# New opening and closing order lists for a fused Linformer attention and feed-forward kernel

## The chip, the core and the metric

The kernel runs on one core of one Trainium2 chip. The metric is device time in microseconds (us) of one execution; lower is better. A profile records one execution: its span runs from the first to the last instruction. The engines are PE (TensorE matmuls), PEld (TensorE weight loads), DVE (VectorE), ACT (ScalarE), POOL (GpSimd, which here mostly issues the input transfers) and SP (which here issues the output and the small internal transfers).

## What is computed

Attention whose keys and values are projected from 1024 positions to 64, and then a feed-forward block on the concatenated heads:

```python
k_proj = einsum('ks,bhsd->bhkd', E, k);  v_proj = einsum('ks,bhsd->bhkd', F, v)
scores = matmul(q, k_proj^T) / sqrt(64)
attn   = softmax(scores, axis=-1)
x      = matmul(attn, v_proj)            # (8, 8, 1024, 64) -> 8192 tokens x 512
h      = x @ w_in                        # 8192 x 2048
out    = (h * sigmoid(1.702 * h)) @ w_out    # 8192 x 512
```

There are 8 batches, 8 heads, 1024 positions and a head size of 64. Inputs and output are float32; the matmuls run in bfloat16.

## The kernel before

**Blocks.** The 8192 tokens are cut into 16 blocks of 512 tokens, numbered 0 to 15. Block j belongs to batch j // 2, so a new batch starts at every even j. Each block goes through attention and then through the two feed-forward products. From block 2 on the first product, and from block 1 on the second, use the Strassen-Winograd scheme: seven half-size products in place of eight, and sums and copies on DVE and ACT between them. Blocks 0 and 1 use plain products where the summed weights are not ready yet.

**Steps.** All work is cut into small named steps. `step(name, j, banks, eng)` emits the instructions of one step for block j. A word such as `xt.0@2:4` means step `xt.0` of block 2 with its result in PSUM bank 4; `/A` or `/D` puts a copy on ACT or on DVE. The steps are:

| step | engine | what it does |
|---|---|---|
| `pj`, `kb`, `kt`, `kc`, `vq`, `vx` | PE, then copies | project keys and values of a new batch, transpose the keys, copy them out |
| `qt`, `qc` | PE, copy | transpose the queries of a block, copy them out |
| `sc`, `ex` | PE, ACT | scores; exponential |
| `tk`, `tr`, `tm`, `xt`, `xc` | PE, DVE, DVE, PE, copy | attention output of blocks 1 and 2, token-major: product, reciprocal, scaling, transpose, copy |
| `su`, `den`, `ga`, `rc`, `sr`, `sb` | PE, copy, SP, DVE, SP, SP | softmax sums of blocks 3 to 15: sum, copy, regroup by DMA (`rc<-den`), reciprocal, write (`rdr<-rc`), broadcast by DMA (`rbc<-rdr`) |
| `va`, `mv` | PE, DVE | attention output of these blocks; scaling by `rbc` |
| `xs` | DVE | sums of the attention output for the first product |
| `L`, `Lg` | PE, ACT | plain first product of block 1; its activation |
| `uN.P1` to `uN.P7`, `uN.c1` to `c3`, `uN.d1`, `d2`, `uN.g11` to `g22` | PE, copies, DVE, ACT | the seven products of quarter N (0 to 3), copies and sums between them, activations |
| `gs` | DVE | sums of the activations for the second product |
| `O`, `oc` | PE, copy | plain second product of block 0; copy to the output tile |
| `F1` to `F7`, `f3`, `f5`, `Fc1` to `Fc3`, `Fo`, `Fd`, `fd2`, `fc3` | PE, copies, DVE | Strassen-Winograd second product; copies and sums |
| `ws`, `wi` | DVE or ACT | sums of the weights `w_out` and `w_in` |
| `gt` | ACT | load the activation table of the feed-forward activation |
| `st*`, `s0` | SP | store output |
| `ld`, `lq` | POOL | load keys and values, or queries, of the next batch |

**Order.** The order is written out in lists. A preamble in code does block 0's attention and first product. After that `listed(OPEN)` emits the 547 words of the list `OPEN`; a loop over j = 4 to 12 emits the list `STEPS`, in which `+n` shifts a step to block j + n; and `listed(TAIL)` emits the 248 words of the list `TAIL`. Each engine executes its own instructions strictly in the order of emission. Across engines an instruction waits only for what it needs: data, or the last reader of a buffer or PSUM bank that it overwrites. So a word's place matters only against other words of the same engine; for the waits, the number of words of other engines ahead of it does.

**The Strassen-Winograd copies.** Within a quarter `uN`, `c1` copies the result of P1 to a second bank before P2 adds onto the first and P6, P7 and P4 add onto the second; `c2` must read that bank between P6 and P7; `c3` must read the third bank between P5 and P3; `d1` must come between P7 and P4. In the second product `Fc1` must copy the first bank after both halves of F1 and before F2 adds onto it. Each of these is a place where PE waits for ACT or DVE.

**Fixed order outside the lists.** POOL's queue holds, after the preamble, `ld@2`, `lq@2`, `ld@4`, `lq@4` and so on: `ld` waits until `pj` of the batch has read the old keys and values, and `lq` until the last `qt` of the batch has read the old queries.

Of the kernel before, what the change touches and what calls it, by code (L numbers as in the profile page):

```python
# [17 lines left out]
def kernel(ctx, tc, q, k, v, E, F,  # L18
# [251 lines left out]
    xs = {}  # L270
# [107 lines left out]
    def ffn2_ops(j):  # L378
# [8 lines left out]
        O.3.0@0:7 wi.4@1 sc.1@1:2,6 sc.0@1:1,0 ex.0.1@1 ex.0.0@1 O.2.0@0:3 O.2.1@0 O.3.1@0 tk.1.0@1:5 ex.1.0@1  # L387
        tk.0.0@1:4 tk.0.1@1:0 O.0.0@0:1 O.1.0@0:2 tr.0.1@1 ex.1.1@1 gt@3 tm.0.1@1 tr.0.0@1 tk.1.1@1:6 O.3.2@0
        tr.1.1@1 O.3.3@0 tm.0.0@1 tk.2.1@1:0 tm.1.1@1 xt.0@1:6 O.0.1@0 tr.2.1@1 tr.1.0@1 tm.1.0@1 tm.2.1@1
        oc.3@0/A xt.1@1:7 tk.2.0@1:5 tk.3.0@1:0 O.0.2@0 xc.0@1/A tr.2.0@1 tm.2.0@1 tk.3.1@1:5 O.2.2@0 O.1.1@0  # L390
        O.2.3@0 tr.3.0@1 ws.0@1 tr.3.1@1 tm.3.0@1 xc.1@1/A tm.3.1@1 ws.2@1 oc.2@0/D xt.3@1:7 xt.2@1:4 O.1.2@0
        ws.1@1 O.1.3@0 xc.2@1/A xc.3@1/A O.0.3@0 L.6@1:5 L.7@1:7 L.8@1:3 oc.1@0/D L.2@1:4 Lg.7@1 Lg.8@1 Lg.6@1
        qt.0@2:6 pj@2:2 oc.0@0/A qc.0@2/A vq.0@2/D L.5@1:5 L.1@1:0 L.11@1:7 L.0@1:3 vq.1@2/A gt@4 Lg.2@1 Lg.5@1
        kb@2/D L.3@1:1 Lg.3@1 L.10@1:6 L.12@1:4 Lg.1@1 Lg.11@1 Lg.0@1 Lg.12@1 L.4@1:0 wi.5@1/D Lg.10@1 vx.0@2
        vx.1@2 Lg.4@1 L.13@1:2 ws.3@1 L.9@1:4 kt@2:7 Lg.13@1 L.15@1:1 ws.4@1 gs3.1@1 kc@2 sc.0@2:3,7 Lg.9@1
        Lg.15@1 qt.1@2:5 ex.0.0@2 s0.0@0 qc.1@2/D ld@2 qt.0@3:2 qt.1@3:4 qc.1@3/D sc.1@2:1,6 ex.1.1@2 tk.0.1@2:4
        ex.0.1@2 ex.1.0@2 gt@1 tk.0.0@2:5 qc.0@3/D tr.0.0@2 L.14@1:6 tk.1.1@2:2 tk.1.0@2:0 tm.0.0@2 tr.0.1@2
        tm.0.1@2 tr.1.0@2 tk.2.0@2:7 Lg.14@1 lq@2 xt.0@2:5 tm.1.0@2 tr.1.1@2 tm.1.1@2 sc.0@3:4,3 tk.3.0@2:0
# [414 lines left out]
```

## Time and profile before

| what | value |
|---|---|
| time, median of 3 runs | 480.43 us (480.08 to 480.87) |
| the profiled execution: time, and its span | 481.29 us, 479.5 us |
| mean granted TensorE clock | 0.999 |
| DVE busy | 347.9 us (73%), 633 instructions |
| ACT busy | 325.1 us (68%), 561 instructions |
| POOL busy | 81.2 us (17%) |
| the word before `OPEN` ends on PE, first PE step of `OPEN` starts | 36.21 us |
| last PE step of `OPEN` ends, `STEPS` starts on PE | 162.47 us |
| `TAIL` starts on PE | 413.41 us |
| last transfer's issue | 476.29 us |

The times of PE steps come from the PE timeline: a group such as eight matmuls of 128x128 by 128x256 is one half of an `F` step. Matmuls are pipelined[...], so the busy share of PE hides short stalls. The distance from the start of one step to the start of the next is the honest cost: `F` starts lie 0.873 us apart in gapless stretches, `P` starts 0.437 us.

### The profile page before, as it was taken

What the parts mean: (1) busy time and instruction counts of PE and PEld (TensorE: products, weight loads), DVE (VectorE), ACT (ScalarE), POOL (GpSimd) and SP (SyncE); (2) the same over time, 40 slices, a digit from 0 to 9 for tenths busy, and PEclk for the clock granted to TensorE, in tenths of its full rate; (3) what the DMA queues carried; (4) which work ended last, traced back from release to release, by engine and by line L of the source; (5) the groups of instructions that cost most, each with busy time, mean ns of one, the idle gap of its engine ahead of it and who ended that gap; (6) DMA issues with size and microseconds to landing.
All of it is one profiled execution on the core that took longest, in us unless ns stands there. A gap on an engine that the chain in (4) does not pass through costs nothing.

```text
span 479.5 us, 11084 instructions
## 1 busy us (share of the span) xinstructions
PE 471.6 (98%) x4613; PEld 375.7 (78%) x4621; DVE 347.9 (73%) x633; ACT 325.1 (68%) x561; POOL 81.2 (17%) x105
## 2 busy tenths in 40 slices
PE   8999999999999999999999999999999999999996
PEld 4644446887878788887888878887888888888885
DVE  4556588578687867869585895958688695959673
ACT  2665389689576867677686757868577777757452
POOL 7562116015000150004200070001400000000000
PEclk9999999999999999999999999999999999999999
DMA  9999999859913299166983299451950505132013
GB/s 163 200 188 203 195 224 140 151 150 167 224 75 90 94 149 251 43 174 43 192 211 87 93 92 235 120 134 47 116 151 23 158 3 134 48 90 89 0 46 133
DMA packets 102390, 61.43 MB, mean 128 GB/s; under 512 B 67524, under 2 KB 91588, under 8 KB 102340
## 3 DMA queue, kind: packets, MB, share of 16 engines
q0 software_dynamic: 86496, 29.37, 54.2%
q1 hardware_dynamic: 15764, 31.10, 22.0%
q8 instruction: 36, 0.59, 0.5%
q10 hardware_dynamic: 80, 0.26, 0.2%
q14 instruction: 14, 0.11, 0.1%
HBM read 72.88 MB, written 16.99 MB: 187 GB/s over the span
## 4 chain that ended last, share of the span: by engine, by line
PE 82%; DMA 11%; DVE 3%; ACT 1%; POOL 1%; issue 1%; SPq 0%; DVEq 0%; ACTq 0%; POOLq 0%
PE k_ps L507 36%; PE k_ps L613 33%; DMA w_out_sb<-in_moe_w_out_dram 3%; PE k_ps L559 3%; PE k_ps L242 2%; PE k_ps L677 2%; DMA v_sb<-in_v_dram 2%; DMA w_in_sb<-in_moe_w_in_dram 2%; DMA rbc<-rdr 2%; PE k_ps L698 2%; PE k_ps L553 2%; DMA rdr<-rc 1%; DVE xT L649 1%; DVE sg L376 1%; PE k_ps L655 1%
## 5 line engine op out<-in xcount | busy, mean ns | idle before, releaser
L492 DVE TENSOR_TENSOR q_even<-k_ps,q_even 128x512 f32<-128x512 f32 x112 | 73.9, 686 | 52.6 <-ACT q_even L619 44.1
L507 PEld LDWEIGHTS <-sg 128*128 128x128 bf16 x960 | 93.6, 98 | 11.6 <-issue 0.9
L613 PEld LDWEIGHTS <-late 128*128 128x128 bf16 x896 | 87.5, 98 | 10.3 <-issue 0.2
L613 PE MATMUL k_ps<-xw,late 128*128 128x256 bf16 x672 | 95.3, 273 | 0.0
L507 PE MATMUL k_ps<-tw,sg 128*128 128x256 bf16 x720 | 88.8, 273 | 0.0
L629 ACT ACTIVATE gT<-q_even 128x512 bf16<-128x512 f32 x112 | 67.8, 629 | 18.8 <-PE k_ps L507 13.7
L507 PEld LDWEIGHTS <-gT 128*128 128x128 bf16 x720 | 69.0, 98 | 12.5 <-issue 4.8
L629 ACT ACTIVATE gT<-k_ps 128x512 bf16<-128x512 f32 x112 | 63.0, 599 | 20.2 <-PE k_ps L613 19.8
L613 PEld LDWEIGHTS <-w_in_sb 128*128 128x128 bf16 x672 | 64.7, 98 | 12.5 <-issue 4.9
L613 PE MATMUL k_ps<-xT,w_in_sb 128*128 128x256 bf16 x448 | 66.1, 273 | 0.0
L70 POOL DMA_DIRECT2D q_sb<-in_q_dram x56 | 49.0, 908 | 79.2 <-PE k_ps L698 69.6
L507 PE MATMUL k_ps<-w_out_sb,gT 128*128 128x256 bf16 x480 | 59.6, 273 | 0.4 <-ACT k_ps L521 0.4
L376 DVE TENSOR_TENSOR sg<-gT 128x1024 bf16<-128x1024 bf16 x60 | 40.6, 683 | 0.4 <-ACT gT L629 0.4
L621 ACT COPY q_even<-k_ps 128x512 f32<-128x512 f32 x40 | 23.5, 589 | 24.3 <-PE k_ps L613 24.0
L641 ACT ACTIVATE expT<-k_ps 128x512 bf16<-128x512 f32 x60 | 32.9, 607 | 7.5 <-PE k_ps L242 7.0
L649 DVE TENSOR_TENSOR xT<-k_ps,rbc 128x512 bf16<-128x512 f32 x52 | 33.0, 682 | 0.9 <-DMA rbc<-rdr 0.8
L613 PE MATMUL k_ps<-xw,w_in_sb 128*128 128x256 bf16 x224 | 33.4, 273 | 0.0
L613 PE MATMUL k_ps<-xT,late 128*128 128x256 bf16 x224 | 33.3, 273 | 0.0
L507 PE MATMUL k_ps<-w_out_sb,sg 128*128 128x256 bf16 x240 | 31.0, 273 | 0.0
L507 PE MATMUL k_ps<-tw,gT 128*128 128x256 bf16 x240 | 29.0, 273 | 0.0
L619 ACT COPY q_even<-k_ps 128x512 f32<-128x512 f32 x36 | 21.5, 598 | 10.7 <-PE k_ps L613 10.6
L712 POOL COPY held<-rbc 1x1 f32<-1x1 f32 x5 | 0.9, 173 | 157.9 <-DMA rbc<-rdr 157.9
(129 smaller groups left out, 602.4 us busy)
## 6 DMA issues: line engine op xcount, KB each, us to landing
out_dram<-o_sb SPq DMA_DIRECT2D x31, 512.0 KB, 3.6
rbc<-rdr SPq DMA_DIRECT2D x26, 512.0 KB, 6.8
k_sb<-in_k_dram POOLq DMA_DIRECT2D x7, 1024.0 KB, 10.8
q_sb<-in_q_dram POOLq DMA_DIRECT2D x56, 128.0 KB, 4.4
v_sb<-in_v_dram POOLq DMA_DIRECT2D x7, 1024.0 KB, 18.5
w_in_sb<-in_moe_w_in_dram POOLq DMA_DIRECT2D x8, 256.0 KB, 10.6
w_out_sb<-in_moe_w_out_dram POOLq DMA_DIRECT2D x4, 512.0 KB, 12.1
v_sb<-in_v_dram POOLq DMA_DIRECT2D x4, 256.0 KB, 10.7
```

What stands on the lines that cost most here:

```text
L70: nc.gpsimd.dma_start(out=qt[b][:, j], in_=qv[:, j])
L242: nc.tensor.matmul(outs[i][r.start + c:r.start + c + w], lhsTs[i][ri, c:c + w], rhss[i][ri], start=True, stop=True)
L376: nc.vector.tensor_tensor(t[i - 1], in0, in1, op=ALU.add if i == 1 else ALU.subtract)
L492: nc.vector.tensor_tensor(out_, in0, in1, op=ALU.add)
L507: nc.tensor.matmul(dst, x[:, k_, t * P:(t + 1) * P], w[:, k_], start=(first and k_ == 0), stop=(final and k_ == FH - 1), skip_group_check= ...
L559: nc.tensor.matmul(h_ps, w_in_sb[:, kc, t * P:(t + 1) * P], xT[j][:, kc, :], start=(kc == 0), stop=(kc == KC - 1))
L613: nc.tensor.matmul(live[h, j][:, r], a[:, k_, f:f + P], w[:, k_], start=(i in (1, 5) and r == 0 and k_ == 0), stop=(i in (2, 3, 4) and r = ...
L619: copy(u1, live[B_, j])
L621: copy(u2, live[G, j])
L629: nc.scalar.activation(out_, in_, AF.Gelu_apprx_sigmoid)
L641: nc.scalar.activation(expT[j][:, 2 * n + t, :], live[f"S{n}{t}", j], AF.Exp, scale=scale)
L649: nc.vector.tensor_tensor(x_of(j)[:, n, :], live[f"V{p[1]}{t}", j], rbc[j][:, n, :], op=ALU.mult)
```

## The change

The lists `OPEN` and `TAIL` are replaced by others. Each holds exactly the same steps of the same blocks as before, 547 and 248 of them. What differs is the order, the PSUM bank that a step is given, and the engine of some copies: in `OPEN` 29 copies go from ACT to DVE and 21 from DVE to ACT, in `TAIL` 8 and 10. `STEPS`, the loop, `step`, the preamble and the bank defaults stay as they are.

The start of `OPEN`, its words up to the middle of block 2's attention, and the last lines of `TAIL`:

```diff
     OPEN = """
-        O.3.0@0:7 wi.4@1 sc.1@1:2,6 sc.0@1:1,0 ex.0.1@1 ex.0.0@1 O.2.0@0:3 O.2.1@0 O.3.1@0 tk.1.0@1:5 ex.1.0@1
-        tk.0.0@1:4 tk.0.1@1:0 O.0.0@0:1 O.1.0@0:2 tr.0.1@1 ex.1.1@1 gt@3 tm.0.1@1 tr.0.0@1 tk.1.1@1:6 O.3.2@0
-        tr.1.1@1 O.3.3@0 tm.0.0@1 tk.2.1@1:0 tm.1.1@1 xt.0@1:6 O.0.1@0 tr.2.1@1 tr.1.0@1 tm.1.0@1 tm.2.1@1
...
-        ws.1@1 O.1.3@0 xc.2@1/A xc.3@1/A O.0.3@0 L.6@1:5 L.7@1:7 L.8@1:3 oc.1@0/D L.2@1:4 Lg.7@1 Lg.8@1 Lg.6@1
-        qt.0@2:6 pj@2:2 oc.0@0/A qc.0@2/A vq.0@2/D L.5@1:5 L.1@1:0 L.11@1:7 L.0@1:3 vq.1@2/A gt@4 Lg.2@1 Lg.5@1
...
-        vx.1@2 Lg.4@1 L.13@1:2 ws.3@1 L.9@1:4 kt@2:7 Lg.13@1 L.15@1:1 ws.4@1 gs3.1@1 kc@2 sc.0@2:3,7 Lg.9@1
-        Lg.15@1 qt.1@2:5 ex.0.0@2 s0.0@0 qc.1@2/D ld@2 qt.0@3:2 qt.1@3:4 qc.1@3/D sc.1@2:1,6 ex.1.1@2 tk.0.1@2:4
-        ex.0.1@2 ex.1.0@2 gt@1 tk.0.0@2:5 qc.0@3/D tr.0.0@2 L.14@1:6 tk.1.1@2:2 tk.1.0@2:0 tm.0.0@2 tr.0.1@2
-        tm.0.1@2 tr.1.0@2 tk.2.0@2:7 Lg.14@1 lq@2 xt.0@2:5 tm.1.0@2 tr.1.1@2 tm.1.1@2 sc.0@3:4,3 tk.3.0@2:0
-        tk.2.1@2:1 xc.0@2/A tr.2.1@2 xt.1@2:6 tm.2.1@2 tr.2.0@2 sc.1@3:2,1 xc.1@2/D ex.0.0@3 s0.1@0 tm.2.0@2
...
+        sc.1@1:6,5 wi.4@1 sc.0@1:4,7 ex.0.1@1 O.2.0@0:1 O.3.0@0:2 O.1.0@0:0 ex.0.0@1 ex.1.0@1 tk.0.0@1:4
+        tk.1.1@1:3 O.3.1@0 tk.0.1@1:7 tk.1.0@1:6 O.1.1@0 tr.0.1@1 tr.0.0@1 tm.0.1@1 wi.5@1/D tr.1.1@1 tm.0.0@1
+        ws.0@1 O.1.2@0 O.2.1@0 tk.2.1@1:7 ex.1.1@1 tm.1.1@1 xt.0@1:4 O.3.2@0 tr.1.0@1 tr.2.1@1 tm.1.0@1 xc.0@1/D
+        tk.2.0@1:5 tr.2.0@1 O.3.3@0 O.1.3@0 O.0.0@0:4 tm.2.0@1 tk.3.1@1:5 tm.2.1@1 xt.1@1:6 tk.3.0@1:3 tr.3.1@1
...
+        O.0.3@0 xt.2@1:2 O.2.3@0 xc.2@1/A oc.0@0/D ws.2@1 L.6@1:0 oc.2@0/A L.1@1:1 L.4@1:7 Lg.1@1 Lg.4@1 Lg.6@1
+        L.11@1:5 L.8@1:3 qt.0@2:7 ws.3@1 qc.0@2/D pj@2:0 Lg.11@1 Lg.8@1 qt.1@2:3 L.5@1:1 L.9@1:5 kb@2/D kt@2:4
+        qc.1@2/D vx.1@2 kc@2 ws.1@1 Lg.5@1 L.3@1:1 sc.0@2:2,4 Lg.9@1 Lg.3@1 ws.4@1 L.7@1:7 ex.0.1@2 L.10@1:3
+        ex.0.0@2 L.2@1:6 gt@2 L.15@1:1 L.13@1:2 Lg.2@1 Lg.13@1 L.0@1:5 vq.1@2/D qt.1@3:4 vq.0@2/D ws.5@1/D
+        vx.0@2 Lg.7@1 Lg.0@1 Lg.10@1 s0.1@0 L.14@1:0 tk.0.0@2:7 qc.1@3/D tk.0.1@2:4 s0.0@0 L.12@1:6 F1.0@1:5
+        Lg.14@1 Lg.15@1 tr.0.1@2 tr.0.0@2 tm.0.1@2 tm.0.0@2 Lg.12@1 sc.1@2:6,1 sc.1@3:4,7 tk.1.1@2:2 gs1.0@1
+        gs1.1@1 qt.0@3:3 qc.0@3/D gs2.0@1 ex.1.0@2 F5.0@1:0 F1.1@1 gs2.1@1 ex.1.1@2 ex.1.1@3 ex.1.0@3 tk.2.0@2:3
+        F5.1@1 tk.1.0@2:6 Fc1@1:1/D xt.0@2:4 tk.2.1@2:7 tr.1.1@2 tm.1.1@2 gs3.1@1 tr.1.0@2 tm.1.0@2 ld@2 F2.0@1
...
+        tr.3.0@2 F6.0@1 tm.3.0@2 xc.1@2/A tm.3.1@2 gs3.0@1 sc.0@3:2,5 Fc2@1/D xc.0@2/D Fc3@1/A ex.0.0@3 ex.0.1@3
+        pj@4:7 su@3:4,2 gs4.1@1 kb@4/D den.0@3/A gs4.0@1 F7.1@1 xt.2@2:5 den.1@3/A xs.0@2 xt.3@2:3 xc.2@2/A
...
     TAIL = """
...
-        u3.g21@15 F1.0@15:0 F1.1@15 u2.g22@15 u3.d2@15 gs1.0@15 u2.g12@15 u3.g12@15 Fc1@15:5/D gs1.1@15 gs2.1@15
-        u2.P4@15 u2.g21@15 F3.0@14 gs2.0@15 F2.0@15 Fd2@14 gs4.1@15 f5.0@15:3 F6.0@15 F6.1@15 gs3.0@15 gs3.1@15
-        st1@14 f5.1@15:6 Fc2@15/A gs4.0@15 F7.1@15 st0@14 F7.0@15 fc3.0@15 fc3.1@15 F2.1@15 f3.0@15 Fo0@15/A
-        Fd1@15 fd2.0@15 F4.1@15 F4.0@15 f3.1@15 st0h@15 st2.0@15 fd2.1@15 Fo1@15/A st1@15 st2.1@15
...
+        u2.c3@15/A u3.g11@15 u3.d1@15 u3.P4@15 u3.P3@15 u2.d1@15 u2.g11@15 u2.P4@15 F1.0@15:5 u3.d2@15 gs1.0@15
+        F1.1@15 u2.P3@15 u3.g21@15 u2.g21@15 u3.g12@15 u3.g22@15 st1@14 st0@14 u2.d2@15 Fc1@15:6/A u2.g22@15
+        u2.g12@15 gs2.0@15 F2.1@15 F2.0@15 gs1.1@15 f5.0@15:1 gs2.1@15 gs4.0@15 gs3.0@15 gs3.1@15 fc3.0@15
+        F6.0@15 F6.1@15 gs4.1@15 f5.1@15:7 Fc2@15/A fc3.1@15 Fo0@15/A F7.0@15 F7.1@15 Fd1@15 f3.1@15 F4.1@15
+        F4.0@15 f3.0@15 fd2.1@15 Fo1@15/A st2.1@15 st0h@15 st1@15 fd2.0@15 st2.0@15
```

In the left-out middle of `OPEN` the PE steps with 32- or 64-wide tiles stand in these runs, where `+` means directly one after the other on PE. Before: `sc.1@1+sc.0@1`, `pj@2`, `sc.0@2`, `sc.1@2`, `sc.0@3`, `sc.1@3`, `pj@4`, `su@3`, `sc.1@4+sc.0@4`, `su@4+va.1@3`, `va.0@3+sc.0@5+pj@6+sc.1@5`, `va.0@4+su@5`, `va.1@4+sc.1@6`, `sc.0@6`, `su@6`, `va.0@5+va.1@5`. After: `sc.1@1+sc.0@1`, `pj@2`, `sc.0@2`, `sc.1@2+sc.1@3`, `sc.0@3+pj@4+su@3`, `sc.0@4+sc.1@4`, `va.0@3+su@4+va.1@3+pj@6`, `sc.0@5+sc.1@5`, `su@5`, `va.0@4+va.1@4`, `sc.1@6+sc.0@6`, `su@6+va.1@5+va.0@5`. In `TAIL` `va.0@15` and `va.1@15` stand apart before and together after.

## The prediction

> **What bounds the kernel.** First the page: engine totals and the chain of waits.
>
> ```profile
> span 479.5 us, 11084 instructions
> ...
> PE 471.6 (98%) x4613; PEld 375.7 (78%) x4621; DVE 347.9 (73%) x633; ACT 325.1 (68%) x561; POOL 81.2 (17%) x105
> ...
> PE 82%; DMA 11%; DVE 3%; ACT 1%; POOL 1%; issue 1%; SPq 0%; DVEq 0%; ACTq 0%; POOLq 0%
> ```
>
> PE is the bound, and the change takes nothing from its work. So the question is how much of PE's time in the two lists is not work. "98% busy" can't tell, because a matmul's printed duration covers a short stall. I therefore read the PE timeline and set the start of each step against the sum of the steps before it. Step prices from gapless stretches: O and L 0.864 us, F 0.873, P 0.437, qt 0.44, xt and kt 0.22, tk 0.11, sc, va and su 0.225, pj 1.72.
>
> One price is hidden: steps in narrow tiles (sc, va, su; pj in another shape).
>
> ```profile
> 132.72 0.60 PE L613 MATMUL k_ps<-xT,late 128*128 128x256 bf16 x4
> 133.25 0.41 PE L242 MATMUL k_ps<-expT,vq 64*32 64x512 bf16 x8
> 133.47 0.40 PE L655 MATMUL k_ps<-expT,ones 64*32 64x512 bf16 x8
> 133.81 1.05 PE L613 MATMUL k_ps<-xw,w_in_sb 128*128 128x256 bf16 x8
> ```
>
> P takes 0.437, but va starts 0.53 later; va to su is 0.22; su to the next P is 0.34. Each change of tile shape costs about 0.105, and two neighbours of one shape pay it once.
>
> Adding up: OPEN holds 119.7 us of steps and 34 changes of shape (3.6), 123.3 in all, and ran from 36.21 to 162.47 = 126.26. So it **stalls 3.0 us**. TAIL: 62.0 of work in 62.2 (413.41 to 475.63, the last matmul's start plus its pitch). Where the 3.0 arise:
>
> ```profile
> 43.84 1.02 PE L553 MATMUL k_ps<-w_out_sb,gT 128*128 128x512 bf16 x4 [0.15 <-DMA w_out_sb<-in_moe_w_out_dram]
> ...
> 56.94 0.40 PE L677 MATMUL k_ps<-k_sb,eft 128*64 128x512 bf16 x1
> 57.38 0.38 PE L677 MATMUL k_ps<-v_sb,eft 128*64 128x512 bf16 x1
> ...
> 71.75 0.40 PE L570 MATMUL k_ps<-vx,expT 128*128 128x130 bf16 x4 [0.53 <-ACT expT L641]
> ...
> 75.12 0.38 PE L585 MATMUL k_ps<-ident,x_sb 128*128 128x128 bf16 x4 [0.50 <-ACT gT L562]
> ...
> 78.40 1.05 PE L507 MATMUL k_ps<-w_out_sb,gT 128*128 128x256 bf16 x8
> ...
> 162.47 1.91 PE L507 MATMUL k_ps<-w_out_sb,gT 128*128 128x256 bf16 x16
> ```
>
> Lag behind the sum of work: 0.5 at O.3.3 (43.84; 0.2 of it earlier at w_out's second quarter, 0.3 here at the fourth), 0.9 after pj@2 (v landed about 57.3), 1.6 at tk.0.1@2 (71.75), 2.6 at xt.1@2 (75.12), 2.8 at F1.0@1 (78.40), and only 3.0 at the end. The last 84 us of OPEN have practically no stall.
>
> The two largest come from ACT's tables:
>
> ```profile
> 69.80 1.28 ACT L641 ACT_TABLE_LOAD   x1
> 71.10 2.06 ACT L641 ACTIVATE expT<-k_ps 128x512 bf16<-128x512 f32 x4
> 73.18 1.28 ACT L255 ACT_TABLE_LOAD   x1
> 74.47 0.60 ACT L562 ACTIVATE gT<-k_ps 128x512 bf16<-128x512 f32 x1
> ```
>
> The exponentials wait for a load, tk waits for them; then Lg.14 waits for the load back, and xt.1@2, in Lg.14's bank, waits for Lg.14.
>
> **Part 1, fewer changes of shape.** New OPEN: 27 (sc@2 and sc@3 together, pj between sc and su, the va together); 7 x 0.105 = **-0.73**. TAIL: 2 instead of 4, **-0.21**. Nothing hides these on PE.
>
> **Part 2, the stalls of OPEN.** I walk the new list: PE's start is 36.21 plus the work ahead; a consumer starts 0.2 after a PE step's issue ends (471.27+0.87 to ACT at 472.34); back to back (groups of two to four in the timelines) ACT takes 0.52 a gelu, 0.50 a copy, 0.48 an exponential, 1.30 a table load; DVE 0.60 a 512-wide sum, 0.42 a tm, 2.29 a large ws or wi.
> - *w_out.* The second to fourth quarter landed at about 38.75 (O.2.1's wait), 41.3 (POOL's next issue at 41.54 less the lag of 0.24 that it has behind PE at the fourth) and 43.8; issues unchanged. First users are now O.3.1 at 39.68, O.1.2 at 41.63, O.3.3 at 44.66. -0.5.
> - *First exponentials.* Ends 38.87, 39.35, 39.83, 40.31; tk.0.0 at 39.46 needs the second. No wait.
> - *xt.0@1* at 43.47: tm.0.0 ends about 43.4, behind wi.5, now on DVE. Edge.
> - *pj@2* at 57.32, v landed about 57.3: 0 to 0.2 instead of 0.4.
> - *sc@2 to tk@2.* Before, tk followed scores within 1 us. Now sc.0@2 is at 62.5 and tk.0.0@2 at 69.3, behind seven L; ACT fits both loads between (ends Lg.3 63.2, load 64.5, two exponentials 65.6, load 66.9, Lg.7 68.5, which frees tk.0.0's bank). The later group: Lg.12 71.2, load 72.5, exponentials to 74.55; their users are at 74.23 (needs the first), 75.2 and 75.3. -1.8 in all.
> - *Edges there:* tk.0.1@2 (69.43, bank freed 69.35), sc.1@2 (71.38, bank freed 71.2), F5.0@1 (72.49, its second sum ready 72.5). Each 0 to 0.2.
> - *Copies.* DVE takes 8 more in OPEN, about 5 us; in 48 to 160 us it has over 25% idle. At su@3 (81.9) its queue has finished xc.0@2 by 81.5. If this cover fails, PE pays the difference.
>
> Stalls left: 0.2 as in the old quiet stretch, plus 0.4 for the edges (ends 0 and 1.2). -3.0 + 0.6 = **-2.4**.
>
> **A rule against it.** The Trainium skill, "ScalarE: Activation LUTs", What ACT_TABLE_LOAD costs: a switch is a load of about 1.28 us plus about 1.38 of drain. Both lists cause 12 loads. With 1.38 more on each, Lg.7 would end at 71.3, two after tk.0.0's turn, and the next load would cost tk.2.0 and xt.0 another 1.3: 3.3 us lost, part 2 undone, and no gain left. The row decides: from the load's start at 69.80 to the exponential at 71.10 is 1.30, with no drain visible before it either (the gelu ahead, 69.19 plus 0.60, ends at 69.79). I take 1.30.
>
> **Part 3, transfers that move.** lq@2 waits for the last qt@3, which moves from about 70.7 to 72.5; POOL issues eight, 7 us, 4.4 to land: 84.5, needed by qt.0@4 at 87.2. Hidden. ld@4 waits for pj@4, which ends about 81.8 instead of 78.5; keys and values are needed only at 104.9. But they now run beside block 3's sums:
>
> ```profile
> 92.36 0.33 SPq L668 DMA_DIRECT2D rdr<-rc  x1
> ...
> 95.40 1.32 SPq L672 DMA_DIRECT2D rbc<-rdr  x2
> ```
> ```profile
> 101.97 0.17 POOL L712 COPY held<-rbc 1x1 f32<-1x1 f32 x1 [21.45 <-DMA rbc<-rdr]
> ```
>
> Before, the load was over at 92 and rbc landed 6.6 after its issue. Now rc@3 and the write come at about 91.5 while the load runs to about 95.5; broadcast at 97, landing 103.6; first user mv.1.1@3 at 105.0. Hidden by 1.4. Ends: 0, and the third rival.
>
> **Part 4, TAIL.** One new wait, close to the end. Fc1@15 is on ACT behind u3.g21, u2.g21, u3.g12, u3.g22. In time from TAIL's start: F1.1 ends 50.9, u2.P3 51.3, then F2.1 wants Fc1. ACT can start Fc1 at 51.1 (F1.1 plus 0.2), ends 51.7: PE waits **0.4** (0 to 0.7); behind it stand F2 to f3. Before, P4 and F3.0@14 lay there. The last sequence, f half, fd2, store, has the same lengths. With part 1 and 0.1 of residue TAIL is 62.3 instead of 62.2: **+0.1**, part 1's 0.21 included. STEPS and the preamble: 0.
>
> **Sum.** OPEN -0.73 - 2.4 = -3.1, TAIL +0.1: -3.0, span 479.5 to 476.5. The profiled execution itself took 481.29, 1.8 beyond its span and 0.9 above the median; the difference applied to the median 480.43 gives **477.4**.
>
> **Rivals.**
> - *The edges give.* Some eight places have margins under 0.3 us. If they and the later ones (va.1@3 and pj@6, banks freed by the last activations of block 2 at 104.1 to 104.7) slip together, 1.6 us come back: 479.0. For: my latencies are good to 0.1 only. Against: 84 equally dense us of the old list lost 0.2.
> - *The stalls move.* PE waits elsewhere for the same 12 loads; only the shapes' 0.9 less TAIL's 0.4 remain: 479.9, within 0.2% (0.96 us, the least that measurement tells from no change). Against: the walk.
> - *Slower: the broadcast of block 3.* The gather under load may take 9.3 (82.67 to 91.99 bounds it), so rc@3 comes at 92.9; the write 6.9 (173.76 to 180.65), the broadcast 11.2 (180.65 to DVE at 191.9): landing 111.3, 6.3 after 105.0. DVE then holds gs and copies, and PE loses some 5: 482.4. It turns the sign from a landing after 108.4. For: those rows exist. Against: they belong to queues with fresh query and key loads; here the load is ending.
>
> **Chances and range.** Forecast 0.62, edges 0.20, moved 0.08, broadcast 0.10. The likeliest's own range is 476.7 to 478.3 (edges 0 to 1.2, Fc1 0 to 0.7); with the edges' rival 476.7 to 479.3. Faster by over 0.2%: 0.62 + 0.20 less 0.01; same 0.09; slower 0.10.
>
> **What would show it.** Right: first L at about 52.5 instead of 52.95; F1.0@1 at 70.4 with no [ACT] wait on tk; OPEN ending near 159.4; TAIL about 62.3 long with an ACT wait at F2.1@15. Wrong: PE waits on ACT in 62 to 76, on DVE mv with rbc as releaser at 105, or OPEN ending after 161.

## The result, and the profile after

| | time, median | runs |
|---|---|---|
| before | 480.79 us (480.08 to 480.97) | 7 |
| after | 479.24 us (478.50 to 480.97) | 7 |

The ratio is 0.9968, with a 95% interval from 0.9953 to 0.9982: 1.55 us faster, where 3.0 were forecast, and 479.24 lies above the forecast's 476.7 to 478.3. The profiled execution of the changed kernel took 480.97 us and was the slowest of its seven; its span is 479.2 us.

The page first: engine totals and the chain of waits.

```profile
span 479.2 us, 11089 instructions
...
PE 469.7 (98%) x4621; PEld 375.5 (78%) x4621; DVE 351.1 (73%) x639; ACT 319.8 (67%) x555; POOL 82.1 (17%) x105
...
PE 83%; DMA 14%; POOL 1%; issue 1%; DVE 0%; SPq 0%; ACT 0%; DVEq 0%; POOLq 0%; ACTq 0%
```

The shares of the chain have moved a little (DVE 3% to 0%, DMA 11% to 14%), but they do not say where. The PE timeline, read against the sum of work as in the prediction, does tell. These are the rows that answer to those of before:

```profile
53.21 4.48 PE L559 MATMUL k_ps<-xT,w_in_sb 128*128 128x512 bf16 x20
...
58.07 0.40 PE L677 MATMUL k_ps<-k_sb,eft 128*64 128x512 bf16 x1
58.59 0.38 PE L677 MATMUL k_ps<-v_sb,eft 128*64 128x512 bf16 x1
...
71.70 1.04 PE L507 MATMUL k_ps<-w_out_sb,gT 128*128 128x256 bf16 x8
...
137.05 0.38 PE L688 MATMUL k_ps<-ident,k_b 128*128 128x128 bf16 x4 [2.03 <-DVE xT L649]
...
162.55 1.91 PE L507 MATMUL k_ps<-w_out_sb,gT 128*128 128x256 bf16 x16
```

The list starts 0.8 us later than in the profile of before (its first scores are at 37.02), and 0.1 of that is in the forecast, a change of shape at its start. PE waited 1.1 us for keys, values and queries ahead of the list, and 0.2 in the profile of before. Allow for the other 0.7, and the first L step at 53.21 has no lag against the forecast 52.5. F1.0@1 at 71.70 has 0.6 against 70.4, 0.5 of it the wait for the values at 58.59. There is no [ACT] wait between 62 and 76, for ACT's timeline now has the switch to the exponentials and back ahead of their users:

```profile
64.50 1.28 ACT L641 ACT_TABLE_LOAD   x1
65.79 1.08 ACT L641 ACTIVATE expT<-k_ps 128x512 bf16<-128x512 f32 x2
66.89 1.28 ACT L255 ACT_TABLE_LOAD   x1
```

So far it is the forecast. Then, at 137.05, comes a wait of 2.03 us that was nowhere in the old list, and the list ends at 162.55, behind the 161 that the prediction gave as a sign of being wrong. The key transposes of block 6 (`kt@6:4`) go to PSUM bank 4, where the attention output of block 4 lies (`va.0@4:1,4`). They wait for the scaling `mv` on DVE that reads it out, and that one waits for the broadcast of block 4's reciprocals. The DVE timeline of after has both broadcasts on which it waits in this list:

```profile
106.72 0.69 DVE L649 TENSOR_TENSOR xT<-k_ps,rbc 128x512 bf16<-128x512 f32 x1 [2.17 <-DMA rbc<-rdr]
...
136.31 0.69 DVE L649 TENSOR_TENSOR xT<-k_ps,rbc 128x512 bf16<-128x512 f32 x1 [2.61 <-DMA rbc<-rdr]
```

Block 3's is late for DVE as well, but PE has other work there and no wait of PE stands there in this profile. Block 4's costs PE 2.03.

Why it is late can be read from the queues of POOL (loads) and SP (write, store, broadcast), first after:

```profile
110.84 7.00 POOL L70 DMA_DIRECT2D q_sb<-in_q_dram  x8 [6.26 <-PE k_ps L698]
117.76 0.95 POOL L58 DMA_DIRECT2D k_sb<-in_k_dram  x1
118.62 0.96 POOL L58 DMA_DIRECT2D v_sb<-in_v_dram  x1
```
```profile
118.22 0.33 SPq L668 DMA_DIRECT2D rdr<-rc  x1
119.75 0.34 SPq L547 DMA_DIRECT2D out_dram<-o_sb  x1
123.64 1.29 SPq L672 DMA_DIRECT2D rbc<-rdr  x2
```

and the same rows before, with the first user of the broadcast:

```profile
106.31 7.00 POOL L70 DMA_DIRECT2D q_sb<-in_q_dram  x8 [4.17 <-PE k_ps L698]
113.24 0.95 POOL L58 DMA_DIRECT2D k_sb<-in_k_dram  x1
114.10 0.95 POOL L58 DMA_DIRECT2D v_sb<-in_v_dram  x1
```
```profile
116.89 0.33 SPq L668 DMA_DIRECT2D rdr<-rc  x1
122.28 1.27 SPq L672 DMA_DIRECT2D rbc<-rdr  x2
```
```profile
133.70 0.69 DVE L649 TENSOR_TENSOR xT<-k_ps,rbc 128x512 bf16<-128x512 f32 x1
```

The load of batch 3's queries (`lq@4`) waits for the last query transposes of batch 2, which stand further back in the new list; so it, and behind it on POOL the keys and values of batch 4 (`ld@6`), go out 4.5 us later. The reciprocals' write goes out only 1.3 us later. The first user would come at the same time: without its idle time DVE would have begun at 136.31 - 2.61 = 133.70, as before. So between write and user there are 15.5 us where there were 16.8, and the 3 MB of loads (1 MB of queries and twice 1 MB) cover all of that stretch. The broadcast took 12.7 us from its issue (123.64 to 136.31). Before, it had loads beside it too, but they ended sooner: the values landed at 132.6 (18.5 us from 114.10) where after they landed at 141.4. Its second half, issued at 122.94, landed 10.1 us later, so it was in place at 133.0, 10.8 us from the first issue.

### The profile page after: what moved, and what is told of

The parts are those of the page before. It is cut to its first block, busy times and chain, and to the rows that moved or that the text cites. A ratio compares the mean times of both kernels' runs of the same rounds, so it can differ in the third digit from the quotient of the medians.

```text
span 479.2 us, 11089 instructions
## 1 busy us (share of the span) xinstructions
PE 469.7 (98%) x4621; PEld 375.5 (78%) x4621; DVE 351.1 (73%) x639; ACT 319.8 (67%) x555; POOL 82.1 (17%) x105
## 4 chain that ended last, share of the span: by engine, by line
PE 83%; DMA 14%; POOL 1%; issue 1%; DVE 0%; SPq 0%; ACT 0%; DVEq 0%; POOLq 0%; ACTq 0%
PE k_ps L507 38%; PE k_ps L613 34%; DMA v_sb<-in_v_dram 6%; PE k_ps L242 3%; PE k_ps L677 3%; DMA rbc<-rdr 2%; DMA w_in_sb<-in_moe_w_in_dram 2%; PE k_ps L698 2%; DMA w_out_sb<-in_moe_w_out_dram 2%; PE k_ps L559 2%; DMA rdr<-rc 1%; PE k_ps L655 1%; POOL k_sb L58 0%; PE k_ps L688 0%; PE k_ps L570 0%
## 5 line engine op out<-in xcount | busy, mean ns | idle before, releaser
L629 ACT ACTIVATE gT<-q_even 128x512 bf16<-128x512 f32 x112 | 68.4, 632 | 13.9 <-PE k_ps L507 12.6
L613 PEld LDWEIGHTS <-w_in_sb 128*128 128x128 bf16 x672 | 64.5, 98 | 12.7 <-issue 5.0
L621 ACT COPY q_even<-k_ps 128x512 f32<-128x512 f32 x37 | 21.7, 588 | 19.5 <-PE k_ps L613 19.5
L619 ACT COPY q_even<-k_ps 128x512 f32<-128x512 f32 x41 | 24.4, 598 | 15.3 <-PE k_ps L613 15.3
## 6 DMA issues: line engine op xcount, KB each, us to landing
k_sb<-in_k_dram POOLq DMA_DIRECT2D x7, 1024.0 KB, 10.9
w_out_sb<-in_moe_w_out_dram POOLq DMA_DIRECT2D x4, 512.0 KB, 11.5
```

Source lines behind the costliest of these rows:

```text
L613: nc.tensor.matmul(live[h, j][:, r], a[:, k_, f:f + P], w[:, k_], start=(i in (1, 5) and r == 0 and k_ == 0), stop=(i in (2, 3, 4) and r = ...
L619: copy(u1, live[B_, j])
L621: copy(u2, live[G, j])
L629: nc.scalar.activation(out_, in_, AF.Gelu_apprx_sigmoid)
```

## Experiments

The theory, called A in the expectations: the shifted loads make the broadcast late, and without that the new opening list brings what was forecast. Rivals: the profiled run was a bad draw (B); the chain of sums, write and issue is late of itself (C); the output store ahead of the broadcast on SP's queue holds it up (S). Each run was timed against the kernel before on the same chip.

**The changed kernel again**, nothing edited.

> The changed kernel once more, nothing edited: how much of the missing 1.5 us is in every run. Theory A (the queries of batch 3 are loaded 4.5 us later, their transfer lies beside the broadcast of block 4's reciprocals, and the broadcast lands late): again about 479.2 us, and in the profile the wait of TensorE at the key transposes of block 6 (k_ps, 2.03 us in the first profile) comes again with 1.5 to 2.5 us. Rival B (the profiled run had a bad start: the opening list began at 36.93 us instead of 36.21, and the late broadcast is of the same kind): that wait is under 0.5 us this time and the median near 478.

479.57 us (9 runs), before 481.15; ratio 0.996 (0.9945 to 0.9974). The list started at 36.25 this time, as before, and the wait came again, smaller:

```profile
135.16 0.38 PE L688 MATMUL k_ps<-ident,k_b 128*128 128x128 bf16 x4 [0.78 <-DVE xT L649]
```

0.78 lies between the two expectations. B is right in that the first profile had a large draw, but the wait is in both, and the median of nine runs misses the forecast by as much as the first seven did.

**The queries of batch 3 in a buffer of their own.**

> The changed kernel with a buffer of their own for the queries of batch 3, so that their load doesn't wait for the last query transposes of batch 2 and issues near 105 us instead of 110.84; the later load of batch 4's queries is held by a read of a block-7 tile so that it doesn't come earlier. Everything else as in the changed kernel. Theory A: the broadcast of block 4 is in place before its first user, the 2.03 us at the key transposes of block 6 fall under 0.3, the time is 1.5 to 2.0 us below the changed kernel, about 477.4. Rival B: the same time as the changed kernel within 0.4 us, and the wait as large or as small as there. Rival C (the broadcast is late for its own chain, from the reciprocals over the write to its issue, not for the loads): the wait stays at 1.5 us or more although the load issues early.

```diff
-        return ldpool.tile([P, J, H, D], BF16, name="q_sb" if b else "q_even")
+        return ldpool.tile([P, J, H, D], BF16, name="q_sb3" if b == 3 else "q_sb" if b else "q_even")
...
         elif i == "lq":
             if b >= 2:
                 nc.gpsimd.tensor_copy(held[:, 0], rbc[max(rbc)][:1, 0, :1])
+            if j == 6:
+                nc.gpsimd.tensor_copy(held[:, 1], qT[7][:1, 2, 0, :1])
```

478.30 us (6 runs), ratio 0.9934 (0.9911 to 0.9957): 2.85 us below before. POOL's and DVE's timelines of this run:

```profile
103.48 7.00 POOL L70 DMA_DIRECT2D q_sb<-in_q_dram  x8
110.41 0.95 POOL L58 DMA_DIRECT2D k_sb<-in_k_dram  x1
```
```profile
132.48 0.69 DVE L649 TENSOR_TENSOR xT<-k_ps,rbc 128x512 bf16<-128x512 f32 x1 [0.21 <-DMA rbc<-rdr]
```

The loads go out 7 us earlier. The broadcast is issued at 122.75, hardly earlier than in the first profile, and is used 9.7 us after that instead of 12.7. DVE waits 0.21, PE not at all. This is as A has it, though smaller: the median is 1.27 below the changed kernel on the same chip (479.57), where 1.5 to 2.0 were expected. C expected the wait to stay.

**The kernel before, with the queries' load late.**

> The kernel before with one thing more: the load of batch 3's queries waits on GpSimd for a tile of block 6's projection, so that it issues about 5 us later than the 106.31 us it had, near 111; the lists of the kernel before are untouched. Theory A: the broadcast of block 4, which had no wait, lands late, and TensorE loses 1 to 2.5 us before the value multiplications or transposes that stand behind it; the time goes from 480.8 to 482 to 483. Rivals B and C: the time is that of the kernel before within 0.4 us.

```diff
         elif i == "lq":
             if b >= 2:
                 nc.gpsimd.tensor_copy(held[:, 0], rbc[max(rbc)][:1, 0, :1])
+            if j == 4:
+                nc.gpsimd.tensor_copy(held[:, 1], vqs[(b + 1) % 2][:1, 0, :1])
             load_q(b + 1)
```

481.10 us (12 runs) against 481.15, ratio 0.9994 (0.9981 to 1.0007): no difference, although the load went out at 113.64, later than meant and later than in the changed kernel. A, as it was put, missed. SP's and DVE's timelines say why:

```profile
117.00 0.33 SPq L668 DMA_DIRECT2D rdr<-rc  x1
120.93 1.26 SPq L672 DMA_DIRECT2D rbc<-rdr  x2
```
```profile
133.81 0.69 DVE L649 TENSOR_TENSOR xT<-k_ps,rbc 128x512 bf16<-128x512 f32 x1
```

The broadcast was slow here too: its second half, issued at 121.58, landed 11.6 us later, so it took 12.3 us in all. But the write ahead of it took 3.9 us (5.4 in the first profile of after), and 3.9 + 12.3 = 16.2 still fits into the 16.8 us that the old list leaves from write to user. It would not fit into the 15.5 of the new list. So late loads alone cost PE nothing here. By this sum it takes both, the loads' company and the 1.3 us less that the new list leaves; no run changes the second alone.

**The new opening list with the old end list.**

> The new opening list with the old end list: what the new end list is worth alone. The prediction had +0.1 us for it (0.4 for the wait of TensorE on a copy that moved to ScalarE, less the two shape changes that it saves). The two profiles had 62.22 us before and 62.50 after from the first matmul of the end list to the last. If the end list costs what the profiles show, this kernel is 0.1 to 0.4 us faster than the changed kernel, near 478.9; if the new end list is a gain, it is slower by up to 0.3 us. The wait for the broadcast of block 4 stays as in the changed kernel.

```diff
     TAIL = """
-        u3.g21@13 u3.g12@13 u2.g12@13 F1.0@13:0 mv.0.0@14 u3.g22@13 ga@15 F1.1@13 mv.1.1@14 xs.0@14 u0.P1@14:7
...
+        ga@15 F1.0@13:0 u3.g12@13 u2.g12@13 mv.0.0@14 u3.g22@13 F1.1@13 xs.0@14 mv.1.1@14 gs1.1@13 gs3.0@13
...
```

479.61 us (12 runs), ratio 0.9967 (0.9947 to 0.9986). The times can't separate this from the changed kernel. The profiles can: from the first score sums of the end list to the last group of matmuls it is 62.57 us with the old list, in this run and in the kernel before, and 62.86 with the new one, in both profiles of it. The new end list costs 0.29.

**The keys and values of batch 4 held until the broadcast has landed.**

> The changed kernel, with the load of batch 4's keys and values (2 MB, issued at 117.8 us) held on GpSimd until the broadcast of block 4 has landed: one small read of the broadcast tile is put into the opening list behind its issue. The queries of batch 3 keep their late place. Theory A (loads that run beside it make the broadcast late): the 512 KB land in 6 to 8 us after their issue instead of 12.5 to 13.4, near 129 us, the wait of TensorE at the key transposes of block 6 (2.03 and 0.78 us in two profiles) is gone, and the time is about 1.3 us under the changed kernel, near 478.3, unless the keys then come late for block 8's projection at 164 us (then a wait there). Rival C (the chain before the broadcast's issue is late of itself, or the output store issued just ahead of it holds it up): it lands as before, the wait stays at 0.8 to 2.0 us and the time is that of the changed kernel.

```diff
+        elif i == "hd":
+            nc.gpsimd.tensor_copy(held[:, 1], rbc[j][:1, 0, :1])
...
-        u3.P2@3 u3.P3@3 u2.P3@3 den.0@5/A qc.1@6/D u3.P4@3 u3.d2@3 u3.g11@3 sb@4 gs3.0@3 qt.0@6:3 va.0@4:1,4
+        u3.P2@3 u3.P3@3 u2.P3@3 den.0@5/A qc.1@6/D u3.P4@3 u3.d2@3 u3.g11@3 sb@4 hd@4 gs3.0@3 qt.0@6:3 va.0@4:1,4
```

477.69 us (477.30 to 477.93, 6 runs), ratio 0.9924 (0.9905 to 0.9944): 3.16 us below before. SP's, POOL's and DVE's timelines:

```profile
120.75 1.26 SPq L672 DMA_DIRECT2D rbc<-rdr  x2
```
```profile
125.74 0.17 POOL L711 COPY held<-rbc 1x1 f32<-1x1 f32 x1 [9.25 <-DMA rbc<-rdr]
125.99 0.88 POOL L58 DMA_DIRECT2D k_sb<-in_k_dram  x1
```
```profile
132.26 0.68 DVE L649 TENSOR_TENSOR xT<-k_ps,rbc 128x512 bf16<-128x512 f32 x1
```

The new read on POOL marks the landing: 5.0 us after the issue, 6.5 before the user, and DVE and PE do not wait for it. The same chain, the same store ahead of it, the same late queries; only the 2 MB are gone from beside it. C and S fall as sufficient causes. The keys are not late at block 8: no wait of PE stands there. In this run the second product of block 1 (F1.0@1) starts where the prediction had it, at 70.4:

```profile
70.36 1.04 PE L507 MATMUL k_ps<-w_out_sb,gT 128*128 128x256 bf16 x8
```

**The output store behind the broadcast.**

> The changed kernel with one step moved: the 512 KB output store of block 2 that SyncE issues at 119.75 us, between the write of the reciprocals and their broadcast, is issued behind the broadcast. Rival S (this store lies ahead of the broadcast in the queue and makes it late): the broadcast lands 2 us or more earlier, the wait at the key transposes of block 6 is under 0.3 us, time near 478.3. Theory A (the loads): the wait stays at 0.8 us or more and the time is that of the changed kernel, 479.2 to 479.6. If both share the DMA, it lands about 1 us earlier and the wait is between 0 and 1 us.

```diff
-        u0.P4@3 u0.g21@3 u2.c3@3/D u3.c3@3/A su@5:4,1 u2.P7@3 u3.P7@3 st0@2 den.1@5/A qt.1@6:3 u2.d1@3 u3.d1@3
-        u3.P2@3 u3.P3@3 u2.P3@3 den.0@5/A qc.1@6/D u3.P4@3 u3.d2@3 u3.g11@3 sb@4 gs3.0@3 qt.0@6:3 va.0@4:1,4
+        u0.P4@3 u0.g21@3 u2.c3@3/D u3.c3@3/A su@5:4,1 u2.P7@3 u3.P7@3 den.1@5/A qt.1@6:3 u2.d1@3 u3.d1@3
+        u3.P2@3 u3.P3@3 u2.P3@3 den.0@5/A qc.1@6/D u3.P4@3 u3.d2@3 u3.g11@3 sb@4 st0@2 gs3.0@3 qt.0@6:3 va.0@4:1,4
```

479.17 us (477.53 to 480.25, 12 runs), ratio 0.9957 (0.994 to 0.9973): the time of the changed kernel. In its profile the broadcast was in time by 0.1 us (its second half, issued at 121.58, landed 10.9 us later, and the user began at 132.59) and PE waited for nothing there, but that execution was the fastest of the twelve (477.53). The median speaks against S as the whole cause. A part of it stays possible, for the broadcast took 11.5 us here and 12.7 to 13.4 with the store ahead, but one profile can't show it, since with the loads beside it the wait differs from run to run (2.03, 0.78, 0.97, 0.29 and 0 in the five profiles of the new opening list with late loads beside the broadcast).

**Own buffer and old end list together.**

> A version meant to beat both kernels: the new opening list with the queries of batch 3 in a buffer of their own, and the old end list. The profiles make it 0.29 us faster than the kernel with the own buffer and the new end list (62.57 against 62.86 us from the last score sums of the steps to the last matmul), so about 478.0 us, 3.1 us below the kernel before (ratio about 0.9935). If the end list were no loss, it would be 478.3 or more.

477.90 us (6 runs), ratio 0.993 (0.9909 to 0.9951), 62.57 us for the end list: as expected.

**The price of a change of tile shape.**

> The price of a change of TensorE's tile shape, measured by itself: in the list of the steady steps the second pair of score matmuls is put behind F2.0 instead of ahead of it, so that the scores of one step lie in two places and every one of the 9 passes has two shape changes more. No work is added. The prediction priced one change at 0.105 us: 9 x 2 x 0.105 = 1.9 us slower than the changed kernel, about 481.2, and the passes take 27.99 us each instead of 27.78. If a change costs nothing (rival: the 0.105 us are paid by the matmuls of this form wherever they stand), the time is that of the changed kernel. A stall from the exponentials that come 0.9 us later would show as a wait of its own.

```diff
-        qc.1+3 sc.0+3 lq+2 gs1.1 gs2.1 gs3.1 xs.0+1 ga+2 sc.1+3 F2.0 u0.P1+1 F6.1 vq.0+4 gs3.0 F6.0 kb+4
+        qc.1+3 sc.0+3 lq+2 gs1.1 gs2.1 gs3.1 xs.0+1 ga+2 F2.0 sc.1+3 u0.P1+1 F6.1 vq.0+4 gs3.0 F6.0 kb+4
```

481.28 us (12 runs), ratio 1.0005 (0.999 to 1.002), 2.1 us above the run with the store behind that it shares its chip with (479.17): the gain of the changed kernel is given back. The PE timeline of one pass, from score sums (L655) to score sums, in the changed kernel:

```profile
245.90 0.41 PE L655 MATMUL k_ps<-expT,ones 64*32 64x512 bf16 x8
...
273.01 0.41 PE L655 MATMUL k_ps<-expT,ones 64*32 64x512 bf16 x8
```

and with the scores split, where L242 in 64*32 stands in two places:

```profile
244.12 0.41 PE L655 MATMUL k_ps<-expT,ones 64*32 64x512 bf16 x8
...
249.17 0.41 PE L242 MATMUL k_ps<-qT,kt 64*32 64x512 bf16 x8
250.49 0.41 PE L242 MATMUL k_ps<-qT,kt 64*32 64x512 bf16 x8
271.46 0.41 PE L655 MATMUL k_ps<-expT,ones 64*32 64x512 bf16 x8
```

A pass takes 27.34 us instead of 27.11 (the expectation had the length of a pass wrong, not the difference). That is 0.23 for two changes, 0.115 each; all steps together took 252.10 us instead of 250.03. No wait of PE stands in them. The 0.105 of the prediction is about right, if anything a little low.

**The control: the hold in the kernel before.**

> The control to the held keys: the same hold, of batch 4's keys and values until the broadcast of block 4 has landed, put into the kernel before. Theory A (in the lists of the kernel before this broadcast is in place before its user, and only the new lists made it late): the profile shows no wait of VectorE on it with or without the hold, and the time stays that of the kernel before within 0.4 us. Rival (the hold is a gain for any list, and says nothing of the change): 1.0 to 1.7 us faster than the kernel before, near 479.5.

The same edit as in the held version, at the place of `sb@4` in the old list. 481.04 us (11 runs) against 480.83, ratio 1.0013 (1.0004 to 1.0021): no gain. The broadcast, issued at 118.47, was seen by POOL's read at 123.50, again 5.0 us later, and stood there for 10 us until its user at 133.51:

```profile
123.50 0.17 POOL L711 COPY held<-rbc 1x1 f32<-1x1 f32 x1 [10.37 <-DMA rbc<-rdr]
```

So the hold is worth nothing for itself; it pays where the broadcast is late, in the new list.

**The exponentials late again.**

> One part of the change undone, on the changed kernel with the held keys: the first exponentials of block 2 and the two function tables around them are put behind four more activations on ScalarE, so that the switch of tables comes just ahead of their user again, as in the kernel before; the order of the matmuls changes by one pair of neighbours only. The prediction had 1.8 us for this place (two table loads of 1.30 us and the exponentials on the path). From the rows of the held version: the four activations end about 67.1 us, a table load of 1.28 and one exponential of 0.55 later it is 69.0, and TensorE is free at 67.1, so it loses 2 us there, 2.8 at most if the second table load is late for the next matmuls as well: 479.7 to 480.5 us. If the switch of tables was covered anyhow (rival), under 0.5 us.

```diff
-        qc.1@2/D vx.1@2 kc@2 ws.1@1 Lg.5@1 L.3@1:1 sc.0@2:2,4 Lg.9@1 Lg.3@1 ws.4@1 L.7@1:7 ex.0.1@2 L.10@1:3
-        ex.0.0@2 L.2@1:6 gt@2 L.15@1:1 L.13@1:2 Lg.2@1 Lg.13@1 L.0@1:5 vq.1@2/D qt.1@3:4 vq.0@2/D ws.5@1/D
-        vx.0@2 Lg.7@1 Lg.0@1 Lg.10@1 s0.1@0 L.14@1:0 tk.0.0@2:7 qc.1@3/D tk.0.1@2:4 s0.0@0 L.12@1:6 F1.0@1:5
-        Lg.14@1 Lg.15@1 tr.0.1@2 tr.0.0@2 tm.0.1@2 tm.0.0@2 Lg.12@1 sc.1@2:6,1 sc.1@3:4,7 tk.1.1@2:2 gs1.0@1
+        qc.1@2/D vx.1@2 kc@2 ws.1@1 Lg.5@1 L.3@1:1 sc.0@2:2,4 Lg.9@1 Lg.3@1 ws.4@1 L.7@1:7 L.10@1:3
+        L.2@1:6 L.15@1:1 Lg.7@1 Lg.10@1 Lg.2@1 Lg.15@1 ex.0.0@2 ex.0.1@2 gt@2 L.0@1:5 L.13@1:2 Lg.13@1 vq.1@2/D qt.1@3:4 vq.0@2/D ws.5@1/D
+        vx.0@2 Lg.0@1 s0.1@0 L.14@1:0 tk.0.0@2:7 qc.1@3/D tk.0.1@2:4 s0.0@0 L.12@1:6 F1.0@1:5
+        Lg.14@1 tr.0.1@2 tr.0.0@2 tm.0.1@2 tm.0.0@2 Lg.12@1 sc.1@2:6,1 sc.1@3:4,7 tk.1.1@2:2 gs1.0@1
...
```

480.08 us (12 runs), ratio 0.9985 (0.9974 to 0.9995): 2.4 us above the held version. ACT's and PE's timelines:

```profile
67.55 0.60 ACT L562 ACTIVATE gT<-k_ps 128x512 bf16<-128x512 f32 x1 [0.33 <-PE k_ps L559]
68.15 1.28 ACT L641 ACT_TABLE_LOAD   x1
69.45 1.09 ACT L641 ACTIVATE expT<-k_ps 128x512 bf16<-128x512 f32 x2
```
```profile
70.09 1.02 PE L559 MATMUL k_ps<-xT,w_in_sb 128*128 128x512 bf16 x4 [1.78 <-ACT expT L641]
```

With the load and the first exponential on its path PE waits 1.78. The load starts as the activation before it ends (67.55 + 0.60 = 68.15) and the exponential follows 1.30 later. The opening list takes 1.95 us longer than in the held version; the rest of the 2.4 between the medians is not explained.

**The held keys with a mended end list.**

> A version meant to beat both kernels: the changed kernel with the held keys, and in the end list the copy Fc1 of block 15 on VectorE instead of ScalarE, with one part product (u2.P4 of block 15) moved behind F1.1, so that 0.44 us more of matmuls lie between F1.1 and F2.1, which waits for this copy. The changed kernel waits 0.44 us there. If that wait goes, the end list takes 62.4 to 62.5 us instead of 62.86 from the score sums to the last matmul, and the time is 477.3 (477.69 with the held keys alone). If the activation that the moved product feeds comes too late, the wait stays in another place and the time is 477.7.

```diff
-        u2.c3@15/A u3.g11@15 u3.d1@15 u3.P4@15 u3.P3@15 u2.d1@15 u2.g11@15 u2.P4@15 F1.0@15:5 u3.d2@15 gs1.0@15
-        F1.1@15 u2.P3@15 u3.g21@15 u2.g21@15 u3.g12@15 u3.g22@15 st1@14 st0@14 u2.d2@15 Fc1@15:6/A u2.g22@15
+        u2.c3@15/A u3.g11@15 u3.d1@15 u3.P4@15 u3.P3@15 u2.d1@15 u2.g11@15 F1.0@15:5 u3.d2@15 gs1.0@15
+        F1.1@15 Fc1@15:6/D u2.P4@15 u2.P3@15 u3.g21@15 u3.g12@15 u3.g22@15 u2.g21@15 st1@14 st0@14 u2.d2@15 u2.g22@15
```

478.00 us (476.86 to 479.38, 6 runs), ratio 0.9945 (0.9929 to 0.996). The end list takes 62.58 us, 0.28 less than the changed one: F2.1@15, which had come 0.44 late behind Fc1@15, comes 0.15 late. The median, between those of the other versions, can't show so little. This profile had a wait of its own further ahead, for the values of block 2:

```profile
59.64 0.38 PE L677 MATMUL k_ps<-v_sb,eft 128*64 128x512 bf16 x1 [1.35 <-DMA v_sb<-in_v_dram]
```

**And the projection of block 2 later.**

> The version with the held keys and the mended end list, and one more order: the projection pj of block 2, whose values' load lands between 57 and 59.6 us, is put behind one query transpose and two L steps, about 2.2 us later on TensorE; the key transposes and scores behind it move with it. In the profiles so far the first value matmul of pj stood 0.0 to 1.76 us behind the first key matmul (0.52 in the changed kernel, 1.76 with the mended end list). If this load is what makes the runs of these versions scatter by 0.6 to 2.5 us, the wait is gone, the values follow the keys at once, the time is 477.2 and the runs lie within 1 us. If the scatter comes from the stage ahead of the opening list (whose end lay between 35.9 and 37.8 us in the profiles), the median is 477.5 to 478.0 and the scatter stays. If the exponentials, which come about 0.9 us later, are then late for the L steps, it is 0.5 us slower.

```diff
-        L.11@1:5 L.8@1:3 qt.0@2:7 ws.3@1 qc.0@2/D pj@2:0 Lg.11@1 Lg.8@1 qt.1@2:3 L.5@1:1 L.9@1:5 kb@2/D kt@2:4
-        qc.1@2/D vx.1@2 kc@2 ws.1@1 Lg.5@1 L.3@1:1 sc.0@2:2,4 Lg.9@1 Lg.3@1 ws.4@1 L.7@1:7 ex.0.1@2 L.10@1:3
+        L.11@1:5 L.8@1:3 qt.0@2:7 ws.3@1 qc.0@2/D Lg.11@1 Lg.8@1 qt.1@2:3 L.5@1:1 L.9@1:5 pj@2:0 kb@2/D
+        qc.1@2/D vx.1@2 Lg.5@1 L.3@1:1 kt@2:4 kc@2 ws.1@1 L.7@1:7 sc.0@2:2,4 Lg.9@1 Lg.3@1 ws.4@1 ex.0.1@2 L.10@1:3
```

478.28 us (478.12 to 480.06, 5 runs), ratio 0.9943 (0.993 to 0.9957): no better than without. The wait for the values is gone, but two new ones stand in the list (0.24 and 0.41 us, the second behind a copy `vx`), and the stretch is 1.4 us longer than in the held version; what the rest of that is, is open. The list began at 37.57, and the view of PE's waits names a reason ahead of the lists (us in all, times, longest):

```profile
PE k_ps L185 <- DMA k_sb<-in_k_dram: 1.9, 1, 1.9
```

**Profiles side by side**, on the PE timeline: where the opening list starts, from there to the first value product of block 5 (its last microsecond is left out), from there to the score sums of the end list, and from these to the last group of matmuls.

| kernel | start | opening list | steps | end list | PE's wait for block 4's broadcast | median less before's, us |
|---|---|---|---|---|---|---|
| before | 36.21 | 125.26 | 250.72 | 62.57 | 0 | |
| before, queries late | 36.12 | 125.47 | 250.35 | 62.56 | 0 | -0.05 |
| before, keys held | 36.60 | 124.69 | 250.36 | 62.57 | 0 | +0.21 |
| after | 37.02 | 124.53 | 250.03 | 62.86 | 2.03 | -1.55 |
| after, again | 36.25 | 123.41 | 250.03 | 62.86 | 0.78 | -1.58 |
| after, old end list | 37.79 | 122.99 | 250.04 | 62.57 | 0.97 | -1.54 |
| after, store behind | 36.19 | 121.81 | 250.13 | 62.86 | 0 | -1.68 |
| after, own buffer | 36.02 | 121.76 | 250.03 | 62.86 | 0 | -2.85 |
| own buffer, old end list | 36.24 | 122.08 | 250.03 | 62.57 | 0 | -2.95 |
| after, keys held | 36.16 | 121.69 | 250.04 | 62.86 | 0 | -3.16 |
| keys held, mended end | 36.84 | 123.41 | 250.03 | 62.58 | 0 | -2.83 |
| the same, projection later | 37.57 | 123.10 | 250.29 | 62.57 | 0 | -2.58 |
| keys held, exponentials late | 37.22 | 123.64 | 250.11 | 62.86 | 0 | -0.75 |
| after, scores split | 36.78 | 122.30 | 252.10 | 62.85 | 0.29 | +0.43 |

The last two rows hold the late exponentials and the split scores, which add a loss of their own, and are left aside here. The other versions of the new list fall into two groups in the last column: 1.5 to 1.7 us where the late loads run beside the broadcast, 2.6 to 3.2 where they are moved out of its way. All five of the second group have medians below those of both kernels; the held version (up to 0.9944) and the own buffer with the old end list (up to 0.9951) also have intervals wholly below that of the changed kernel (from 0.9953). Among themselves the five can't be told apart.

## Why the prediction was half right

**Part 1, changes of shape: right.** The split scores measure 0.115 a change against the 0.105 used; so the seven saved in the opening list are worth 0.7 to 0.8.

**Part 2, the stalls of the opening list: right.** In the held version the list takes 121.69 us in the measure of the table, 3.57 less than in the first profile of the old list and 3.0 less than in the last; parts 1 and 2 promised 3.1. No wait on w_out, on the first exponentials or around the tables is left. Putting the exponentials back behind the activations cost 1.95 us in the list and 2.4 in time, against the 1.8 of the step *sc@2 to tk@2*. The row (1.30 for a switch) was right, and the drain of 1.38 on top, of the prediction's rule against it, does not show here: in three profiles the exponential starts 1.29 or 1.30 behind the load's start, and the load as the activation before it ends. The eight copies more on DVE stayed covered. Mis-sized: *pj@2*, priced at 0 to 0.2. The first value product came 0.5 behind the first key product in the first profile, 0 to 0.4 in nine others, and 1.8 in one, where the row prints a wait of 1.35.

**Part 3, transfers that move: here it failed.** It walked lq@2, ld@4 and block 3's broadcast, found it "Hidden by 1.4", and stopped. Block 3's was in fact later than said (DVE idle until 106.72 instead of a landing at 103.6). The load beside it was sized too short: the values had landed at 94.0 before (14.4 us from 79.62), not "over at 92", and landed at 98.3 after (13.9 from 84.44), not at 95.5. PE did not wait for it in the first profile. The chain that costs time is the next one round: *lq@4*, *ld@6* and block 4's broadcast, which the sum passed over at 0. Its parts were all in the profile of before: the load waits for the last query transposes of batch 2, which the new list puts further back; and the broadcast of the old list took 10.8 us and had 0.7 us of margin (in place at 133.0, used at 133.70), although no wait showed it. The price is 0.3 to 2.0 us in the profiles where it came, and 0.9 to 1.6 in the medians (the two groups of the table). That is the missing half: in the two versions that take this out and leave both lists' order as it is, the gain is 2.85 and 3.16 where 3.0 was forecast. That they meet 3.0 so closely has some luck in it, for the end list and the steps moved by 0.2 to 0.3 against the sum and cancel.

The prediction's own rival "the broadcast of block 3" had the mechanism: a write and a broadcast slowed by loads beside them. It had it one block too early, and at 5 us too dear; it was called unlikely because the load "is ending" there, and at block 4 it is not.

A rule of the Trainium skill would have pointed to the broadcasts: "DMA: Bandwidth & Descriptors", Issuing engines are not separate DMA queues, says that transfers started by different engines run on the same 16 DMA engines and interleave. The runs agree: the broadcast took 5.0 to 5.2 us without the keys and values beside it and 12.7 to 13.4 beside loads that POOL had issued.

The rival "the edges give" had the number, 479.0 against the measured 479.24, but by luck: its places, with margins under 0.3 us, were to slip together. The held version has all of them in it, and its list is as short as the forecast or shorter, so they did not slip.

**Part 4, TAIL: right in kind, too small in size.** The wait of 0.4 at F2.1@15 came, 0.44 late against the matmuls before it (the row of after prints 0.28):

```profile
464.70 1.91 PE L507 MATMUL k_ps<-w_out_sb,gT 128*128 128x256 bf16 x16 [0.28 <-ACT k_ps L521]
```

A second lag that wasn't foreseen, 0.13 at F4.1@15, helps to make the end list 0.29 longer instead of 0.1. Moving the copy and one product takes 0.28 of it off again.

**STEPS and the preamble: 0** held nearly: the steps take 250.0 to 250.3 us with the new opening list, 250.35 and 250.36 in two profiles of the old one, and 250.72 in the first, which had a wait of 0.36 of its own. So most profiles of the new list gain 0.3 there that the sum did not have. The preamble is the same code and still moved the profiled execution by 0.7.

## What to carry to other kernels

When an order is changed, follow every queue through the whole stretch, not only where the first transfers move: a load that waits for the last reader of a buffer goes with that reader, and what it then runs beside pays. A transfer that no one waits for has a margin that the profile doesn't print; work it out as the time from its issue to its first user less what it takes under load. And judge a new order by several executions: two profiles of the same kernel had 2.03 and 0.78 us of this wait.

## What the runs showed of the hardware

- The broadcast (two transfers of 512 KB on SP) landed 5.0 to 5.2 us after its first issue in all five versions that held the 2 MB of keys and values back. Beside the late loads it took 12.7 to 13.4 in the four profiles where DVE waited for it, and 11.5 and 12.3 in two others.
- The 16 KB write ahead of it took 1.8 us, up to the broadcast's issue, with only the end of the query loads beside it (118.47 less 116.71, the kernel before with held keys; the last query load landed at 117.39) and 3.4 to 6.0 in the others. In eight of these 13 profiles it landed 0.16 to 0.18 us behind the last of the eight query loads; why is open.
- Behind the same code ahead of them, the lists began anywhere between 36.0 and 37.8 us in the 14 profiles. PE's wait for the first keys in that code was 0 to 2.2 us, and 2.2 and 1.9 in the two that began last. So two single executions can differ by up to 1.8 us ahead of the lists.
